# A two-layer attention kernel: value banks opened at the first value product, probabilities in order, the last key chunk token-major, matmul transposes at the barriers, roots of the layer norm on GpSimd

## The chip, the cores and the metric

The kernel runs on one core of one Trainium2 chip. The metric is the device time of one execution in microseconds (us). Every kernel was run four times. Of each the median is given, and a ratio to the kernel before, which was run in the same rounds on the same chip. A 95% interval of the ratio stands in square brackets.

The names in the profile are PE (TensorE, matrix products), PEld (its weight loads, which overlap products), ACT (ScalarE), DVE (VectorE), POOL (GpSimd) and SPq (the queue that issues most transfers). In the lines of the profile D and G are tiles in PSUM, the memory into which TensorE writes its products, X holds the residual, WA and WB are weights, and names that begin with p are tiles of the kernel's pools in SBUF, the on-chip memory for operands.

## The reference

There are two layers, and each is two blocks with a residual. Block A is causal attention in four segments of 512 tokens with 32 heads of 16 columns, plus a running memory. Block B is linear attention with a softmax feature map.

```python
x = x + A(layernorm(x));  x = x + B(layernorm(x))          # twice, x is [2048, 512]
# A, for each segment s of 512 tokens and each head:
p     = softmax(q_s @ k_s.T * 16**-0.5 + causal_mask)
a_dot = p @ v_s
a_mem = (phi(q_s) @ M) / (phi(q_s) @ z + 1e-6)
o_s   = g * a_mem + (1 - g) * a_dot
M, z  = M + phi(k_s).T @ v_s,  z + sum(phi(k_s))
# B, for each head; not causal: kv needs the keys of all 2048 tokens
phi_k = [softmax(k @ w_phi), softmax(-(k @ w_phi))]        # phi_q likewise
kv    = phi_k.T @ v;   z = sum(phi_k)
o     = (phi_q @ kv) / (phi_q @ z + 1e-6)
# layernorm: (x - mean) / sqrt(var + 1e-5), no weights
```

B's sum `kv` is a barrier. No query of B can be finished before the last token of A has gone through the residual, the layer norm and the key side of B. There is one such barrier in each layer.

## The kernel before

The kernel is a Python program that records operations with an estimated duration each. It plans them once, before the launch, and emits one fixed order of instructions for each engine. **The order of each engine stays as planned, whatever the real durations are.** A buffer is taken when the plan issues the first operation that "opens" it, and it comes free after its last reader. `CAPG` limits how many PSUM banks a class may hold at once: `pv` is the value tiles, `gen` the general ones.

```python
CAPG = {"gen": 3, "pv": 2, "nz": 1}

def ln(self, t, xT, flex=False):                    # layer norm of one tile of 128 tokens
    v(lambda e: e.bn_stats(...), 602, ...)          # DVE; the number is the plan's estimate in ns
    v(lambda e: e.bn_aggr(...), 75, ...)            # DVE
    # the root: exp(-0.5 * ln(var + eps)), two operations on ScalarE
    self.g.op({"act": (141.0, lambda e: e.activation(rs, self.mv[:, t, 1:2], ACT.Ln, bias=self.epsln[:, 0:1]))}, ...)
    self.g.op({"act": (141.0, lambda e: e.activation(rs, rs, ACT.Exp, scale=-0.5))}, ...)
    ...                                             # xn = (x - mean) * rstd on DVE
    self.tr(...)                                    # transpose of xn by DMA

def a_att(self, L, s, i):                           # attention of one tile of queries
    for hp in range(2):
        PV = self.T(self.pG, "pv")                  # one value tile: 16 heads, one PSUM bank
        for gg in range(2):
            for j in range(i + 1):
                # scores of 8 heads against 128 keys: two products of 512 columns
                self.mm(..., [512] * 2, ..., [S], opens=[PT, PV], label="S")
                self.act(..., ACT.Exp, 1024, [S], [PT], scale=0.25, label="exp")
                ...                                 # mask of the diagonal tile on GpSimd
            # ... value products, 17 columns each, from PT into PV
    ...                                             # divide, out-projection, residual
```

The key side of B (`b_keys`) works on a chunk of 512 tokens at once. It makes keys feature-major (one feature per partition, the tokens in a row), takes exponentials, transposes them by DMA, and then forms the values and `kv`. With the last chunk all of that lies behind the last token of A.

Of the kernel before, what the change touches and what calls it, by code (L numbers as in the profile page):

```python
# [9 lines left out]
ALU = mybir.AluOpType  # L10
# [470 lines left out]
class Kernel:  # L481
# [50 lines left out]

    def recip(self, e, o, i):

        with self.nc.allow_low_precision(reason="one softmax weight per key and head, kept in the operands' type"):
            return e.reciprocal(o, i)  # L536
# [6 lines left out]
    def alloc(self):  # L543
        nc, sb = self.nc, self.sb
        self.X = sb("X", [128, NT, D], BF16)
        self.WA = {k: sb(f"WA_{k}", [128, 4, D], BF16) for k in ("q", "k", "v", "o")}
        self.WB = {k: sb(f"WB_{k}", [128, 4, D], BF16) for k in ("q", "k", "v", "o")}
        self.ident = sb("ident", [128, 128], BF16)
        self.onesb = sb("onesb", [128, 128], BF16)
        self.eps8 = sb("eps8", [128, 8], BF16)  # L550
        self.epsln = sb("epsln", [128, 1], F32)
        self.ones8 = sb("ones8", [128, 8], F32)
        self.H8 = sb("H8", [128, 8], F32)
        self.H8b = sb("H8b", [128, 8], BF16)
        self.S4 = sb("S4", [128, 4], F32)
        self.A8 = sb("A8", [128, 8], F32)
        self.beta_sb = sb("beta_sb", [128, H], BF16)
        self.gt = sb("gt", [128, 3, H], F32)
        self.GAm = sb("GAm", [128, NG, 8, 17], F32)
        self.MS32 = sb("MS32", [128, NG, 8, 17], F32)  # L560
        self.MSb = [sb(f"MSb{b}", [128, NG, 8, 17], BF16) for b in range(3)]
        self.stats = sb("stats", [128, NT, 6], F32)
        self.mv = sb("mv", [128, NT, 2], F32)
        self.rstd = sb("rstd", [128, NT], F32)
        self.nb = sb("nb", [128, NT], F32)
        self.KV32 = sb("KV32", [128, 8, 136], F32)
        self.Rkv = sb("Rkv", [128, 8, 8, 16], BF16)
        self.Rz1 = sb("Rz1", [128, 8, 8, 2], BF16)
        self.wphi_st = sb("wphi_st", [128, NG, 16], BF16)

        def pool(name, n, shape, dt, caps=None, fifo=()):
            p = Pool(name, [sb(f"{name}{i}", shape, dt) for i in range(n)])
            p.caps = caps or {}
            p.fifo = fifo
            return p
        self.pX = pool("pX", N_XT, [128, 4, 512], BF16, {}, ("xA", "xB"))
        self.pQ = pool("pQ", N_Q4, [128, 4, 512], BF16, {}, ("Q4",))
        self.pK = pool("pK", N_KT, [128, 2, 512], BF16, {}, ("KT",))
        self.pV = pool("pV", 2, [128, 4, H, 17], BF16, {}, ("VT",))
        self.p1 = pool("p1", N_K1, [128, 512], BF16, CAP1, ("QT", "phiQ", "PhK", "phiKT", "E"))  # L580
        self.p2 = pool("p2", N_K2, [128, 1024], BF16, CAP2, ("ET", "EQ"))
        self.pT = pool("pT", N_VT, [128, 2, H, 17], BF16, {}, ("Vt",))
        self.pS = pool("pS", N_SM, [128, 256], F32)
        dbl = [self.es.enter_context(nc.psum_tensor(f"D{i}", [128, 1024], F32)) for i in range(2)]
        sgl = [self.es.enter_context(nc.psum_tensor(f"G{i}", [128, 512], F32)) for i in range(4)]
        self.pD = Pool("pD", dbl, psum=True)
        self.pG = Pool("pG", sgl, psum=True)
        self.pG.caps = CAPG
        self.pools = [self.pK, self.pX, self.pQ, self.pV, self.p1, self.p2, self.pT, self.pS, self.pD, self.pG]
# [5 lines left out]
    def setup(self):  # L595
# [34 lines left out]
        P = "pool"  # L630
        v(lambda e: e.memset(self.ones8[:], 1.0), 120, [], [R("ones8")], eng=P)
# [17 lines left out]
        v(lambda e: e.memset(self.epsln[:], LN_EPS), 70, [], [R("epsln")])  # L649
# [18 lines left out]
        for k in ("q", "k"):  # L668
            for g in range(NG):
                for hf in range(2):  # L670
                    c0 = g * 128 + hf * 64
                    self.evac(lambda k=k, c0=c0: self.WA[k][:, :, c0:c0 + 64].rearrange("p t (d s) -> p t d s", s=4),
                              lambda k=k, c0=c0: self.WAraw[k].t[:, :, c0:c0 + 64].rearrange("p t (s d) -> p t d s", s=4),
                              256, [self.WAraw[k]], [R("WP", k, g, hf)])
# [45 lines left out]
    def ln(self, t, xT, flex=False):  # L720
# [4 lines left out]

        rs = self.rstd[:, t:t + 1]
        self.g.op({"act": (141.0, lambda e: e.activation(rs, self.mv[:, t, 1:2], ACT.Ln, bias=self.epsln[:, 0:1]))},  # L727
                  [R("mv", t), R("epsln")], [R("rstd", t)], label="rstd")
        self.g.op({"act": (141.0, lambda e: e.activation(rs, rs, ACT.Exp, scale=-0.5))}, [R("rstd", t)], [R("rstd", t)], label="rstd")  # L729
# [12 lines left out]
        self.tr(lambda: xT.t[:, :, tt * 128:(tt + 1) * 128], lambda: xn.t[:], [xn], [xT[tt]], label="xnT")  # L742
# [84 lines left out]
    def a_att(self, L, s, i):  # L827
# [9 lines left out]
        for hp in range(2):  # L837
            PV = self.T(self.pG, "pv")
            pvv = lambda PV=PV: PV.t[:, 0:288].rearrange("p (h c) -> p h c", c=18)
            for gg in range(2):  # L840
# [3 lines left out]
                for j in range(i + 1):  # L844
# [5 lines left out]
                        [512] * 2, [KT[0], KT[1]] + Q4all(Q4), [S], opens=[PT, PV], label="S")  # L850
# [15 lines left out]
                if s >= 1:  # L866
# [4 lines left out]
                        [8, 8], [PQ, R("MSb", mb, hp), R("onesb"), R("eps8")], [PV[("d", gg)]], label="NMd")  # L871
# [13 lines left out]
        self.out_proj(t, o, [o[0], o[1]], self.WA["o"], R("WA", "o"))  # L885

    def out_proj(self, t, o, ores, W, wres, store=False, res_pe=False):
        R = self.R
        oT = self.T(self.p1, "oT")
        ps = self.T(self.pG, "gen")  # L890
        self.tr(lambda: oT.t[:].rearrange("p (a b) -> p a b", a=4), lambda: o.t[:], ores, [oT], label="otr")
# [12 lines left out]

    def b_keys(self, L, c):
        R, v = self.R, self.v
# [20 lines left out]
        for tt in range(4):  # L927
# [4 lines left out]
            ps = self.T(self.pG, "gen")  # L932
            self.vproj(ps, self.WB["v"], [R("WB", "v"), Vt["z"]], tt, xT, label="BV")
            v(lambda e, ps=ps, Vt=Vt: e.tensor_tensor(Vt.t[:, :, :, 0:16],  # L934
                                                      ps.t[:, None, 0:512].to_broadcast([128, 2, 512]).rearrange("p s (h d) -> p s h d", h=H),
                                                      Vt.t[:, :, :, 16:17].to_broadcast([128, 2, H, DH]), ALU.mult), 1131,
              [ps[0], Vt["z"]], [Vt["v"]], label="Vt")
        for q in range(3):
# [6 lines left out]
            n = len(slots)  # L945
            src = lambda ps=ps, n=n: ps.t[:, 0:136 * n].rearrange("p (k c) -> p k c", k=n)
            dst = lambda slots=slots, n=n: self.KV32[:, slots[0]:slots[0] + n, :]
            rd = [ps[0]]
            if c == 0:
                v(lambda e, src=src, dst=dst: e.tensor_copy(dst(), src()), 65 + 136 * n / 0.96, rd, [R("KV32", q)], label="KVacc")  # L950
            else:
                v(lambda e, src=src, dst=dst: e.tensor_tensor(dst(), dst(), src(), ALU.add), 65 + 136 * n / 0.96, rd + [R("KV32", q)],
                  [R("KV32", q)], label="KVacc")
            if c == 3:
                s0 = slots[0]
                kv = lambda s0=s0, n=n: self.KV32[:, s0:s0 + n, :].rearrange("p k (h c) -> p k h c", c=17)
                v(lambda e, kv=kv, s0=s0, n=n: e.tensor_tensor(self.Rkv[:, s0:s0 + n], kv()[:, :, :, 0:16],
                                                               self.H8[:, None, :, None].to_broadcast([128, n, 8, 16]), ALU.mult),
                  65 + 128 * n / 0.96, [R("KV32", q), R("H8")], [R("Rkv", q)], label="Rkv")
                v(lambda e, kv=kv, s0=s0, n=n: e.tensor_tensor(self.Rz1[:, s0:s0 + n, :, 0], kv()[:, :, :, 16],  # L960
                                                               self.H8[:, None, :].to_broadcast([128, n, 8]), ALU.mult),
                  90, [R("KV32", q), R("H8")], [R("Rz", q)], label="Rkv")

    def b_query(self, L, c, store):
# [36 lines left out]
        for tt in range(4):  # L1001
# [3 lines left out]
            o = self.T(self.p1, "o")  # L1005
# [3 lines left out]
                    [128] * 8, list(EQ.values()) + [R("Rkv", q) for q in range(3)], [N], opens=[Tm, o], label="N")  # L1009
# [4 lines left out]
            v(lambda e, Tm=Tm, o=o: e.tensor_tensor(o.t[:], Tm.t[:, 0:512], Tm.t[:, 512:1024], ALU.add), 335, [Tm], [o], label="nadd")  # L1014
            self.out_proj(t, o, [o], self.WB["o"], R("WB", "o"), store=store, res_pe=True)


    def build(self):
# [4 lines left out]
        def lnA(L, s):  # L1023
            self.xA[(L, s)] = self.T(self.pX, "xA")
            for t in range(s * 4, s * 4 + 4):
                self.ln(t, self.xA[(L, s)], flex=(L == 1))

        for L in range(2):
# [7 lines left out]
            for s in range(NSEG):  # L1036
# [7 lines left out]
                for i in range(4):  # L1044
                    self.a_att(L, s, i)
                    self.ln(s * 4 + i, self.xB[(L, s)])
                self.b_keys(L, s)
# [22 lines left out]
CAPG = {"gen": 3, "pv": 2, "nz": 1}  # L1070
ROUNDS = 5
# [38 lines left out]
```

## Time and profile before

The kernel before took 661.0 us (median of four runs in the rounds with the changed kernel, 658.42 to 666.8). Its profiled execution has a span of 654.6 us. I cut that span at four events, all read from the timeline: the first projection, the last value product of each layer, and the first normalising multiplication of B's query side in each layer, an operation of VectorE. Between the last value product and that multiplication lies the barrier.

| stage (us) | length |
|---|---|
| head: start to first projection | 21.1 |
| attention of layer 0 | 234.1 |
| barrier of layer 0 | 37.7 |
| queries of B, then attention of layer 1 | 267.5 |
| barrier of layer 1 | 36.7 |
| tail: queries of B of layer 1 | 57.5 |

This is part 1 of the page of the kernel before, busy time of each engine:

```profile
PE 548.8 (84%) x5728; PEld 292.3 (45%) x5728; DVE 433.0 (66%) x901; ACT 480.9 (73%) x705; POOL 157.1 (24%) x155
```

The table of engine time by stretch of the kernel before gives, for each stage after the head, its length, the busy time of each engine with the number of instructions, and the granted clock of TensorE (the number after the POOL entry):

```profile
core 0: us, PE busy (x) PEld busy (x) DVE busy (x) ACT busy (x) POOL busy (x), PEclk, DMA share, GB/s
21.10:255.20 234.10, 209.80 (x2317) 112.29 (x2318) 157.04 (x333) 201.44 (x287) 70.54 (x65) 0.96 0.31 64
255.20:292.90 37.70, 28.32 (x270) 15.48 (x266) 23.26 (x41) 12.93 (x18) 0.00 (x0) 0.91 0.35 64
292.90:560.40 267.50, 242.08 (x2581) 127.94 (x2582) 183.16 (x392) 228.82 (x333) 70.53 (x64) 0.98 0.28 53
560.40:597.10 36.70, 25.55 (x252) 14.38 (x250) 23.04 (x41) 9.03 (x14) 0.00 (x0) 0.91 0.38 69
```

In the barrier nothing is full. These lines are from the timeline of the kernel before, the barrier of layer 0: start, duration, engine, line, operation, count, and in brackets the idle time before it with the releaser.

```profile
254.85 0.40 PE L508 MATMUL G<-pV,p 128*128 128x17 bf16 x10
...
261.11 1.03 PE L508 MATMUL G<-WA_o,p 128*128 128x512 bf16 x4
...
265.38 0.29 ACT L727 ACTIVATE rstd<-mv,epsln 128x1 f32<-128x1 f32 x1 [3.92 <-DVE mv L724]
265.62 1.02 ACT L514 ACTIVATE p<-D 128x1024 bf16<-128x1024 f32 x1
266.54 0.19 ACT L729 ACTIVATE rstd<-rstd 128x1 f32<-128x1 f32 x1
...
267.51 0.40 DVE L739 TENSOR_SCALAR p<-X,mv,rstd 128x512 bf16<-128x512 bf16 x1
...
270.72 3.61 PE L508 MATMUL D<-pX,WB_k 128*128 128x512 bf16 x16 [0.73 <-DMA pX<-p]
...
277.78 6.55 PE L508 MATMUL G<-WB_v,pX 128*128 128x512 bf16 x16 [0.66 <-DVE pT L536]
...
285.74 2.05 PE L508 MATMUL G<-pT,p 128*128 128x136 bf16 x32 [1.41 <-DVE pT L934]
...
289.00 0.96 PE L508 MATMUL G<-Rz,p 128*128 128x16 bf16 x32 [1.21 <-DVE Rz L960]
```

From the last value product to the first sum of the queries (`Rz`) it takes 33.8 us (255.2 to 289.0). The second half of the root, at 266.54, queued behind an exponential of something else. The 16 value projections at 277.78 took 6.55 us, 0.41 us each, about twice the densest pitch, at a granted clock of 0.5. The Trainium skill, "TensorE: Matmul & The Clock Gate", Part 1, says that the array falls to half its clock after an idle window of about 3.4 us; the trace agrees in the size of the step.

Last come the exponentials of the attention of layer 0, from the groups of instructions of the kernel before in 21.1 to 255.2 us: count, busy time, mean ns of one, then the idle time before them and what ended it.

```profile
L514 ACT ACTIVATE p<-D 128x1024 bf16<-128x1024 f32 x171 | 165.7, 1032 | 19.5 <-PE D L508 18.9
```

ScalarE waited 18.9 us in this stretch for scores.

### The profile page before, as it was taken

What the parts mean: (1) busy time and instruction counts of PE and PEld (TensorE: products, weight loads), DVE (VectorE), ACT (ScalarE), POOL (GpSimd) and SP (SyncE); (2) the same over time, 40 slices, a digit from 0 to 9 for tenths busy, and PEclk for the clock granted to TensorE, in tenths of its full rate; (3) what the DMA queues carried; (4) which work ended last, traced back from release to release, by engine and by line L of the source; (5) the groups of instructions that cost most, each with busy time, mean ns of one, the idle gap of its engine ahead of it and who ended that gap; (6) DMA issues with size and microseconds to landing.
All of it is one profiled execution on the core that took longest, in us unless ns stands there. A gap on an engine that the chain in (4) does not pass through costs nothing.

```text
span 654.6 us, 13817 instructions
## 1 busy us (share of the span) xinstructions
PE 548.8 (84%) x5728; PEld 292.3 (45%) x5728; DVE 433.0 (66%) x901; ACT 480.9 (73%) x705; POOL 157.1 (24%) x155
## 2 busy tenths in 40 slices
PE   0479888898899999668998888989897999876885
PEld 0224444544545555334554434544453555334442
DVE  8666867767665764577799767756563776556454
ACT  4479979898887998305888979999898789421532
POOL 6321324333323421000002333333222342000000
PEclk9969989999999999988999999999999999887978
DMA  5923322212510422423333422212321241341323
GB/s 125 313 61 66 62 52 59 43 33 65 75 33 17 71 46 42 72 42 60 71 77 79 80 49 49 53 34 53 80 29 25 34 66 27 74 72 38 70 75 87
DMA packets 129006, 41.83 MB, mean 64 GB/s; under 512 B 120080, under 2 KB 127792, under 8 KB 128944
## 3 DMA queue, kind: packets, MB, share of 16 engines
q1 hardware_dynamic: 127584, 36.21, 28.5%
q0 software_dynamic: 1360, 4.74, 2.3%
q8 instruction: 45, 0.74, 0.5%
q14 instruction: 17, 0.14, 0.1%
HBM read 6.32 MB, written 2.10 MB: 13 GB/s over the span
## 4 chain that ended last, share of the span: by engine, by line
PE 49%; ACT 25%; DVE 15%; DMA 7%; issue 2%; POOL 1%; SPq 1%; ACTq 0%
PE G L508 30%; ACT p L514 22%; PE D L508 19%; DMA p<-p 3%; DVE p L1010 3%; DMA pX<-p 2%; DVE pT L934 2%; DVE p L739 1%; POOL p L854 1%; DMA pQ<-p 1%; DVE stats L723 1%; DVE p L757 1%; DVE pK L522 1%; DVE pT L536 1%; ACT pS L514 1%
## 5 line engine op out<-in xcount | busy, mean ns | idle before, releaser
L514 ACT ACTIVATE p<-D 128x1024 bf16<-128x1024 f32 x384 | 373.1, 1030 | 82.8 <-PE D L508 80.9
L854 POOL TENSOR_SCALAR_AFFINE_SELECT p<-p 128x1024 bf16<-128x1024 bf16 x128 | 140.7, 1104 | 395.7 <-ACT p L514 395.6
L508 PE MATMUL D<-pQ,pK 128*128 128x512 bf16 x640 | 185.5, 386 | 21.8 <-ACT p L514 17.1
L508 PEld LDWEIGHTS G<-pV,p 128*128 128x128 bf16 x2656 | 85.4, 96 | 36.4 <-POOL p L854 11.7
L508 PE MATMUL G<-pV,p 128*128 128x17 bf16 (+1 forms) x2656 | 90.0, 173 | 8.6 <-POOL p L854 5.8
L508 PEld LDWEIGHTS D<-pQ,pK 128*128 128x128 bf16 x640 | 48.3, 98 | 88.9 <-ACT p L514 54.9
L508 PE MATMUL G<-pX,WA_k 128*128 128x512 bf16 x128 | 34.5, 395 | 24.0 <-DMA pX<-p 21.1
L536 DVE RECIPROCAL pS<-G 128x32 f32<-128x32 f32 (+1 forms) x64 | 20.5, 321 | 37.4 <-PE G L508 37.0
L723 DVE BATCH_NORM_STATS2 stats<-X 128x6 f32<-128x512 bf16 x64 | 43.4, 681 | 1.5 <-ACT X L521 0.4
L900 DVE TENSOR_TENSOR X<-X,G 128x512 bf16<-128x512 bf16 x32 | 21.9, 686 | 33.6 <-PE G L508 33.6
L934 DVE TENSOR_TENSOR pT<-G,pT 128x1024 bf16<-128x1024 f32 x32 | 38.5, 1214 | 7.0 <-PE G L508 6.7
L508 PE MATMUL G<-WA_o,p 128*128 128x512 bf16 x128 | 34.1, 390 | 6.2 <-DMA p<-p 4.0
L508 PE MATMUL G<-WA_v,pX 128*128 128x512 bf16 x128 | 35.1, 403 | 4.9 <-ACT p L521 2.3
L508 PE MATMUL G<-WB_v,pX 128*128 128x512 bf16 x128 | 36.8, 433 | 2.3 <-DVE pT L536 2.3
L508 PE MATMUL D<-pX,WB_q 128*128 128x512 bf16 x128 | 35.4, 425 | 4.0 <-DVE p L1010 3.6
L1010 DVE TENSOR_TENSOR p<-D,pS 128x1024 bf16<-128x1024 f32 x32 | 37.8, 1215 | 0.3
L739 DVE TENSOR_SCALAR p<-X,mv,rstd 128x512 bf16<-128x512 bf16 x48 | 26.2, 552 | 16.9 <-ACT rstd L729 16.9
L522 DVE CAST pK<-G 64x512 bf16<-64x512 f32 x42 | 28.9, 687 | 10.8 <-PE G L508 6.3
L508 PE MATMUL G<-WB_o,p 128*128 128x512 bf16 x128 | 34.8, 396 | 0.0
L727 ACT ACTIVATE rstd<-mv,epsln 128x1 f32<-128x1 f32 x64 | 18.6, 295 | 19.7 <-DVE mv L724 19.5
L508 PE MATMUL G<-pX,WA_q 128*128 128x512 bf16 x128 | 32.3, 386 | 0.1
L536 DVE RECIPROCAL pT<-G 128x64 bf16<-128x64 f32 x32 | 17.9, 559 | 21.3 <-PE G L508 20.9
(110 smaller groups left out, 683.1 us busy)
## 6 DMA issues: line engine op xcount, KB each, us to landing
pQ<-p SPq DMA_DIRECT2D x128, 32.0 KB, 1.8
p<-p SPq DMA_TRANSPOSE x152, 2.5
out_dram<-X SPq DMA_DIRECT2D x16, 128.0 KB, 1.7
X<-in_A_x_dram POOLq DMA_DIRECT2D x3, 512.0 KB, 8.7
pX<-p SPq DMA_TRANSPOSE x64, 2.5
pX<-in_B_wqkv_dram POOLq DMA_DIRECT2D x2, 512.0 KB, 8.7
X<-in_A_x_dram SPq DMA_DIRECT2D x4, 128.0 KB, 2.5
pX<-in_A_wk_dram SPq DMA_DIRECT2D x1, 512.0 KB, 3.9
```

Source lines behind the costliest of these rows:

```text
L508: ins = e.matmul(out_ap, lhsT, rhs, start=st, stop=sp, tile_position=(basep(lhsT), basep(out_ap)))
L514: return self.g.op({"act": (dur, lambda e: e.activation(out_ap(), in_ap(), func, scale=scale))}, reads, writes, opens, label=label)
L522: "dve": (n / 0.96 + 65, lambda e: e.tensor_copy(out_ap(), in_ap()))}
L536: return e.reciprocal(o, i)
L723: v(lambda e: e.bn_stats(self.stats[:, t, :], self.X[:, t, :]), 602, [R("X", t)], [R("st", t)], label="bn")
L727: self.g.op({"act": (141.0, lambda e: e.activation(rs, self.mv[:, t, 1:2], ACT.Ln, bias=self.epsln[:, 0:1]))}, [R("mv", t), R("epsln")], [ ...
L739: v(lambda e: e.tensor_scalar(xn.t[:], self.X[:, t, :], self.mv[:, t, 0:1], self.rstd[:, t:t + 1], op0=ALU.subtract, op1=ALU.mult), 300, [ ...
L757: v(lambda e: e.tensor_scalar(e_.t[:], e_.t[:], 1.0, None, op0=ALU.min), 202, [e_], [e_], label="phmin")
L854: v(lambda e, pt8=pt8: e.affine_select(pt8(), pt8(), [[0, 8], [1, 128]], ALU.is_ge, 0.0, base=0, channel_multiplier=-1), 1080, [PT], [PT], ...
L900: self.v(lambda e: e.tensor_tensor(self.X[:, t, :], self.X[:, t, :], ps.t[:, 0:512], ALU.add), 602, [R("X", t), ps[0]], [R("X", t)], label ...
L934: v(lambda e, ps=ps, Vt=Vt: e.tensor_tensor(Vt.t[:, :, :, 0:16], ps.t[:, None, 0:512].to_broadcast([128, 2, 512]).rearrange("p s (h d) -> ...
L1010: v(lambda e, tt=tt, N=N, Tm=Tm: e.tensor_tensor(Tm.t[:].rearrange("p (s h d) -> p s h d", s=2, h=H), N.t[:].rearrange("p (s h d) -> p s h ...
```

## The change

Its intent has five parts. (1) A value bank is opened at the first value product and no longer at the first score product, so scores and exponentials can run ahead. To keep this safe from deadlock, probabilities (`PT`) and value banks are taken in program order. (2) The last chunk of B's keys is made token-major, in two parts, tokens 0 to 383 and then 384 to 511, so that only the last tile should be left behind the barrier. (3) On the latency chains, transposes are done by TensorE with a copy out of PSUM, not by DMA. (4) The roots of the layer norm move from ScalarE to GpSimd, as an add and a power. (5) Weights are permuted group by group, in the order in which the first projections use them.

```diff
     def ln(self, t, xT, flex=False, pe=False):
-        self.g.op({"act": (141.0, lambda e: e.activation(rs, self.mv[:, t, 1:2], ACT.Ln, bias=self.epsln[:, 0:1]))},
-                  [R("mv", t), R("epsln")], [R("rstd", t)], label="rstd")
-        self.g.op({"act": (141.0, lambda e: e.activation(rs, rs, ACT.Exp, scale=-0.5))}, [R("rstd", t)], [R("rstd", t)], label="rstd")
+        v(lambda e: e.tensor_scalar(rs, self.mv[:, t, 1:2], LN_EPS, None, op0=ALU.add), 100,
+          [R("mv", t)], [R("rstd", t)], eng="pool", label="rstd")
+        v(lambda e: e.tensor_tensor(rs, rs, self.mhalf[:], ALU.pow), 120,
+          [R("rstd", t), R("mhalf")], [R("rstd", t)], eng="pool", label="rstd")
...
+        if pe:
+            self.tpe(dst, lambda: xn.t, [xn], [xT[tt]], [xT], label="xnT")   # 4 PE transposes and a copy
+        else:
+            self.tr(dst, lambda: xn.t[:], [xn], [xT[tt]], label="xnT")
...
-        self.p2 = pool("p2", N_K2, [128, 1024], BF16, CAP2, ("ET", "EQ"))
+        self.p2 = pool("p2", N_K2, [128, 1024], BF16, CAP2, ("ET", "EQ", "PT"))
+        self.pG.fifo = ("pv",)
...
-                        [512] * 2, [KT[0], KT[1]] + Q4all(Q4), [S], opens=[PT, PV], label="S")
+                        [512] * 2, [KT[0], KT[1]] + Q4all(Q4), [S], opens=[PT], label="S")
...
+    def b_keys_tok(self, L, c, parts):
+        for part in parts:
+            for tt in part:
+                self.vproj(S, self.WB["k"], [...], tt, xT, opens=[E, Z], label="BK")
+                for sgn in range(2):
+                    self.act(..., ACT.Exp, 512, ..., label="kexp")
+                    v(fn, 598, [E[sgn]], [Z[sgn]], label="Zred")      # sum over the 16 columns of a head
+                ...                                                   # reciprocal, value products, scaling
+            for q in range(3):
+                self.mm(..., label="KV")                              # kv of this part, then added
...
+TOK = {3: ((0, 1, 2), (3,))}
+PE_T = ({("xA", 0, t) for t in range(4)} | {("xB", L, 15) for L in range(2)} | {("a", L, 15) for L in range(2)}
+        | {("b", 0, t) for t in range(4)} | {("xA", 1, t) for t in range(4)} | {("b", 1, 0), ("b", 1, 15)})
```

Cut are the helper of the PE transposes, the pair form of the last out-projections (transpose and sum in one product), and the loop order of the permutes.

## The prediction

> **What bounds it.** The table of engine time by stretch shows two regimes. In the attention stretches (50-257 us and 345-558 us) ScalarE is busy 184 of 207 us and 191 of 213 us; four back-to-back 128x1024 exponentials take 3.68 us (timeline), 0.92 us each, and 320 of them are 294 of those 420 us. TensorE busy is about as high (190 and 192 us) but inflated by pipelining: dense pairs of 512-column products start 0.22 us apart, so it has slack. Around the barriers (257-310, 558-601) and in the tail no engine is full: it is a latency chain at a granted clock of 0.87-0.88. Value products run 0.43 us apart there, twice the dense pitch. The Trainium skill, "TensorE: Matmul & The Clock Gate", Part 1, says an idle stretch of about 3.4 us halves the clock; this trace agrees.
>
> **Barrier (twice).** From the last value product (255.3 us): DMA transpose of o, Wo, LN, DMA transpose of xn (2.5 us each plus issue), 16 key products, exponentials and sums, 16 cold value products, 4 Vt of 1.2 us, 32 KV products, done at 287.7. The change leaves only token tile 15 after the barrier: 4+4 products, 2 half exponentials (0.61 us), 2 reductions (0.65 us each, estimate from same-sized DVE work), a reciprocal 0.56, one Vt, 8 KV products. The key part falls from 17 us to about 8. Two PE transposes with evacuation (4 transposes 0.4 us, copy 0.4-0.6) save some 1.5 us each; roots on Pool stop queueing behind key exponentials (Ln at 265.38, Exp at 266.54). The work for tiles 12-14 moves into busy attention. Net gain about 10 us per barrier, 20 in all.
>
> **Head.** First product waits to 21.1 us for a DMA transpose that took 6.8 us while loads ran. PE transposes plus group-ordered permutes bring it to about 16; the Q4 DMAs still meet the loads. Gain 4 us. Risk: Pool memsets (1.8 us each, 3.6-8.9 us) stand before the roots.
>
> **Layer boundary and tail.** Transposes of x and of the first and last outputs: 4 us together.
>
> **Attention.** A root pair costs ScalarE about 0.29 us of issue spacing, not its 0.50 us of durations; 44 pairs in the attention stretches give 13 us. Not opening the value bank at S lets S and exp run ahead and frees a bank for projections: ScalarE waits for S 34 us there; I expect 8-10 us back. Minus some 6 us of work moved in: net gain 16 us.
>
> Sum: 20+4+4+16 = 44 us.
>
> **Predicted time 617 us**, 80% range 600 to 639; faster by over 2% 0.93, within 2% 0.06, slower 0.01.
>
> **What the profile would show.** Barrier: first query sums 10 us sooner after the last value product, granted clock above 0.9, KV products in groups of 24 and 8. Head: first projection at 15-17 us. Attention: ScalarE 92% or more busy, no roots on it, each stretch 7-9 us shorter, exp waiting for S well below 34 us; Pool has 128 more instructions under 0.5 us. Tail: the last product follows the last nmul without a DMA.
>
> **What would make it wrong.** A slow power on Pool (1 us or more), or roots stuck behind masks in Pool's order. The Trainium skill, "SBUF — State Buffer", Who interferes with whom, says Pool and VectorE lock a shared port; the trace fits it (two xn took 2.70 us while a Pool memset ran, normally 0.55 each). Probabilities in order may cost freedom. The static schedule is rebuilt whole, so a few us may shift anywhere. If attention is bound by the exp-mask-value chain rather than ScalarE, the 16 us shrink to a few.

## More of the kernel before

In the attention stages TensorE is busy for 90% of the time (209.80 of 234.10) and ScalarE for 86% (201.44). Both figures overstate the load, because a record is longer than the time after which its engine starts the next instruction. At its densest, TensorE starts 512-column products 0.216 us apart, while a single record of one is 0.38 us long. I therefore count TensorE work another way: each weight load stands for a product, and each product is charged its densest pitch in the trace (0.216 us for 512 columns, 0.026 us for 17). By that estimate the attention of layer 0 holds 188 us of TensorE work in 234 us (80%), and the following stage holds 223 us in 267.5 us (83%). ScalarE is about as full by a like estimate: its exponentials of 1024 columns have records of 1.03 us and start 0.90 us apart at the densest, so the 171 of layer 0's attention come to 154 us, and with the 36 us of its other records to 190 us in 234 (81%).

## The result and the profile after

The changed kernel took 633.91 us (629.29 to 634.63), with a ratio of 0.9564 [0.9485, 0.9643] to the kernel before. A ratio compares the fast runs of both kernels round by round, so it is not quite the ratio of the medians. The gain is 27 us by the medians and 21.8 us by the two profiled spans (654.6 and 632.8). The stages add up to the spans, so the 21.8 us are what the tables split.

| stage (us) | before | after | difference | predicted |
|---|---|---|---|---|
| head | 21.1 | 15.9 | −5.2 | −4 |
| attention of layer 0 | 234.1 | 237.6 | +3.5 | −7 to −9 |
| barrier of layer 0 | 37.7 | 23.0 | −14.7 | −10 |
| queries, attention of layer 1 | 267.5 | 274.3 | +6.8 | −7 to −9, and part of the −4 below |
| barrier of layer 1 | 36.7 | 23.0 | −13.7 | −10 |
| tail | 57.5 | 59.0 | +1.5 | part of −4 |

The latency chains gained more than predicted. The attention, which was to give 16 us, cost 10 us.

This is part 1 of the page after, and then from part 5 of that page the groups of the roots and of the operation that waits for them:

```profile
PE 535.4 (85%) x5680; PEld 301.4 (48%) x5760; DVE 461.3 (73%) x932; ACT 466.9 (74%) x586; POOL 211.3 (33%) x285
...
L741 POOL TENSOR_SCALAR rstd<-mv 128x1 f32<-128x1 f32 x64 | 15.6, 246 | 151.8 <-DVE mv L739 151.2
...
L754 DVE TENSOR_SCALAR p<-X,mv,rstd 128x512 bf16<-128x512 bf16 x48 | 32.9, 688 | 16.0 <-POOL rstd L743 15.4
...
L743 POOL TENSOR_TENSOR rstd<-rstd,mhalf 128x1 f32<-128x1 f32 x64 | 37.8, 594 | 4.1
```

The power took 594 ns of GpSimd and the add 246 ns, where the plan of the change counted 120 and 100. ScalarE lost 119 instructions and 14 us of busy time. The records of 80 of 5760 products are missing (x5680 against x5760 loads), which is why products are counted by their loads here.

The table of engine time by stretch after, cut at the same events:

```profile
core 0: us, PE busy (x) PEld busy (x) DVE busy (x) ACT busy (x) POOL busy (x), PEclk, DMA share, GB/s
15.90:253.50 237.60, 214.12 (x2394) 119.67 (x2426) 184.18 (x375) 198.96 (x237) 100.24 (x129) 0.98 0.35 73
253.50:276.50 23.00, 14.62 (x140) 8.77 (x137) 14.54 (x33) 7.84 (x12) 0.79 (x2) 0.76 0.00 1
276.50:550.80 274.30, 247.81 (x2681) 139.37 (x2722) 204.97 (x414) 223.75 (x278) 95.45 (x126) 0.97 0.29 52
550.80:573.80 23.00, 14.58 (x138) 8.72 (x135) 14.51 (x34) 7.80 (x12) 0.79 (x2) 0.76 0.00 1
```

ScalarE is now busy for 84% and 82% of the attention stages (86% both times before), and for 89% from 60 to 253 us, a stretch more like the one that I predicted 92% for. TensorE has 108 and 140 more weight loads there (2318 to 2426, 2582 to 2722). At the densest pitch the added products are 12 and 11 us of work by the estimate above. VectorE gained 27 and 22 us of busy time.

The timeline of the barrier of layer 0 after, to be laid beside the one of before:

```profile
252.60 0.96 PE L508 MATMUL G<-pV,p 128*128 128x17 bf16 x32
...
256.05 0.39 PE L540 MATMUL G<-ident,p 128*128 128x128 bf16 x4
...
257.67 1.03 PE L508 MATMUL G<-WA_o,p 128*128 128x512 bf16 x4
...
261.03 0.22 POOL L741 TENSOR_SCALAR rstd<-mv 128x1 f32<-128x1 f32 x1 [9.02 <-DVE mv L739]
261.33 0.57 POOL L743 TENSOR_TENSOR rstd<-rstd,mhalf 128x1 f32<-128x1 f32 x1
261.93 0.41 DVE L754 TENSOR_SCALAR p<-X,mv,rstd 128x512 bf16<-128x512 bf16 x1 [0.99 <-POOL rstd L743]
262.40 0.40 PE L540 MATMUL G<-ident,p 128*128 128x128 bf16 x4 [1.96 <-DVE p L754]
...
263.32 1.04 PE L508 MATMUL G<-WB_k,pX 128*128 128x512 bf16 x4 [0.52 <-DVE pX L522]
...
266.99 1.89 PE L508 MATMUL G<-WB_v,pX 128*128 128x512 bf16 x4 [2.64 <-DVE pT L548]
...
270.20 1.09 PE L508 MATMUL G<-pT,p 128*128 128x136 bf16 x8 [1.32 <-DVE pT L963]
...
272.53 1.02 PE L508 MATMUL G<-Rz,p 128*128 128x16 bf16 x32 [1.24 <-DVE Rz L955]
```

From the last value product (253.6) to the first `Rz` product it is now 19.0 us, 14.8 us sooner than before. On the chain that decides are now only four key products, four value projections and eight `kv` products. Four value projections and 24 `kv` products of the first part also come after the last value product (254.3 to 259.6), but they fill the wait for the last tile. The last value projections still run cold. The table by stretch, cut finer inside this barrier, shows when the clock falls:

```profile
262.40:265.00 2.60, 1.43 (x8) 0.53 (x8) 0.42 (x1) 0.76 (x2) 0.00 (x0) 1.00 0.00 0
265.00:267.00 2.00, 0.01 (x1) 0.01 (x1) 1.88 (x3) 0.60 (x1) 0.00 (x0) 0.65 0.00 0
267.00:269.00 2.00, 1.88 (x4) 0.42 (x4) 0.08 (x1) 0.00 (x0) 0.00 (x0) 0.50 0.00 0
```

It drops to 0.50 during the sums and the reciprocal, and it stays there to the end of the barrier. The mean clock of the barrier fell from 0.91 to 0.76, although I had predicted above 0.9. This goes with a TensorE that is busy for less of the barrier (14.62 of 23.00 us, 64%, against 28.32 of 37.70 us, 75%). That this is the cause was not tested.

The exponentials of the attention of layer 0 after, from the groups in 15.9 to 253.5 us:

```profile
L514 ACT ACTIVATE p<-D 128x1024 bf16<-128x1024 f32 x173 | 168.2, 1029 | 25.0 <-PE D L508 24.1 <-PE G L508 0.2
```

The wait for scores rose from 18.9 to 24.1 us, where I had predicted a clear fall.

### The profile page after: what moved, and what is told of

The parts are those of the page before. It is cut to its first block, busy times and chain, and to the rows that moved or that the text cites. A ratio compares the mean times of both kernels' runs of the same rounds, so it can differ in the third digit from the quotient of the medians.

```text
span 632.8 us, 13820 instructions
## 1 busy us (share of the span) xinstructions
PE 535.4 (85%) x5680; PEld 301.4 (48%) x5760; DVE 461.3 (73%) x932; ACT 466.9 (74%) x586; POOL 211.3 (33%) x285
## 4 chain that ended last, share of the span: by engine, by line
PE 42%; DVE 34%; ACT 9%; POOL 6%; DMA 5%; issue 3%; SPq 0%; POOLq 0%
PE G L508 24%; PE D L508 16%; ACT p L514 7%; DVE p L1086 3%; DMA p<-p 3%; DVE stats L738 3%; DVE pK L522 3%; DVE p L754 3%; DVE p L782 3%; POOL rstd L743 2%; DVE X L933 2%; DVE p L776 2%; POOL p L873 1%; DVE p L893 1%; DVE p L522 1%
## 5 line engine op out<-in xcount | busy, mean ns | idle before, releaser
L514 ACT ACTIVATE p<-D 128x1024 bf16<-128x1024 f32 x376 | 366.9, 1030 | 75.6 <-PE D L508 73.2
L508 PE MATMUL D<-pQ,pK 128*128 128x512 bf16 x640 | 181.8, 382 | 13.6 <-ACT p L514 6.7
L741 POOL TENSOR_SCALAR rstd<-mv 128x1 f32<-128x1 f32 x64 | 15.6, 246 | 151.8 <-DVE mv L739 151.2
L514 ACT ACTIVATE p<-G 128x512 bf16<-128x512 f32 x64 | 38.8, 607 | 8.6 <-PE G L508 4.1
L754 DVE TENSOR_SCALAR p<-X,mv,rstd 128x512 bf16<-128x512 bf16 x48 | 32.9, 688 | 16.0 <-POOL rstd L743 15.4
L522 DVE CAST pK<-G 64x512 bf16<-64x512 f32 x52 | 35.5, 684 | 6.0 <-PE G L508 5.3
L743 POOL TENSOR_TENSOR rstd<-rstd,mhalf 128x1 f32<-128x1 f32 x64 | 37.8, 594 | 4.1
L508 PE MATMUL G<-WB_v,pX 128*128 128x512 bf16 x114 | 31.5, 396 | 7.6 <-DVE pT L548 5.3
L508 PE MATMUL G<-WA_v,pX 128*128 128x512 bf16 x119 | 32.4, 402 | 3.1 <-DVE nb L748 1.2
L508 PE MATMUL D<-pX,WB_q 128*128 128x512 bf16 x122 | 31.2, 393 | 3.2 <-DVE p L1086 3.0
```

What stands on the lines that cost most here:

```text
L508: ins = e.matmul(out_ap, lhsT, rhs, start=st, stop=sp, tile_position=(basep(lhsT), basep(out_ap)))
L514: return self.g.op({"act": (dur, lambda e: e.activation(out_ap(), in_ap(), func, scale=scale))}, reads, writes, opens, label=label)
L522: "dve": (n / 0.96 + 65, lambda e: e.tensor_copy(out_ap(), in_ap()))}
L743: v(lambda e: e.tensor_tensor(rs, rs, self.mhalf[:], ALU.pow), 120, [R("rstd", t), R("mhalf")], [R("rstd", t)], eng="pool", label="rstd")
L754: v(lambda e: e.tensor_scalar(xn.t[:], self.X[:, t, :], self.mv[:, t, 0:1], self.rstd[:, t:t + 1], op0=ALU.subtract, op1=ALU.mult), 300, [ ...
```

## The experiments

Twelve kernels were run, four in each of three calls. The medians of the kernel before in the three were 662.46, 662.61 and 659.21 us. Where kernels of different calls are compared, differences below some 4 us are not read. Two theories stood against each other for the attention.

- **The TensorE theory.** TensorE is the limit there: the moved work costs what it weighs, and relieving ScalarE gives nothing.
- **The GpSimd theory.** The roots on GpSimd hurt by themselves and hide the gain, through the shared port that the prediction names, or through their place in an order that was planned with too short an estimate.

Both can hold a part, so the runs are to tell how much each holds. The expectations are quoted as they were before each run, with the names and guesses of that moment. The first four runs undo one part of the change each.

### Roots back on ScalarE (u_roots)

```diff
-        v(lambda e: e.tensor_scalar(rs, ..., op0=ALU.add), 100, ..., eng="pool")
-        v(lambda e: e.tensor_tensor(rs, rs, self.mhalf[:], ALU.pow), 120, ..., eng="pool")
+        self.g.op({"act": (141.0, ... ACT.Ln, bias=self.epsln ...)}, ...)
+        self.g.op({"act": (141.0, ... ACT.Exp, scale=-0.5 ...)}, ...)
```

> The change with the roots on ScalarE again. My prediction's reckoning: 44 root pairs at 0.29 us come back on ScalarE in attention, so about 10 us slower, 640 to 646 us. Theory M: ScalarE is not what holds attention, so within 4 us of the changed kernel. Theory P (the roots on Pool cost as much as they free: power 0.59 us each where the schedule counts 0.12, and VectorE's normalising op 0.69 us on average against 0.55): a few us faster, 625 to 632 us.

It took 620.58 us (615.96 to 621.63), ratio 0.9357 [0.93, 0.9414]. With the roots back on ScalarE the kernel is 13 us faster than with them on GpSimd. By stages of its profile, the barriers are 4.0 and 3.6 us longer than after the change. In layer 0 the roots' queue on ScalarE explains about 1.5 us of this: from the end of the variance to the normalisation of the last tile it takes 2.5 us (253.0 to 255.6), against 1.0 us after the change (260.9 to 261.9). Most of the rest is key-side work that this order leaves behind the last value product, as the barrier holds 185 weight loads against 134. The head is 3.7 us shorter (12.2), and the two attention stages are 5.4 and 13.3 us shorter (232.2 and 261.0). So the offload, predicted at +13 us, was worth −13 with the plan as written.

### Value bank opened at the scores again (u_open)

```diff
-                        ..., [S], opens=[PT], label="S")
+                        ..., [S], opens=[PT, PV], label="S")
-        ..., CAP2, ("ET", "EQ", "PT"))        # and self.pG.fifo = ("pv",) is gone
+        ..., CAP2, ("ET", "EQ"))
```

> The change with the value bank opened at S and probabilities in any order again. My prediction's reckoning: 8 to 10 us come back, 642 to 646 us, all of it in the attention stretches, where exp waits more for S. Rival (running ahead is worth little because TensorE is full): within 4 us. Rival (running ahead is what pays for the moved work): 15 us or more slower.

It took 681.58 us (680.62 to 683.75), ratio 1.0298 [1.0235, 1.0361]: 48 us slower than the changed kernel and slower than the kernel before. All of it is in the attention (269.9 and 288.7 us). Barriers, head and tail are within 0.2 us of those after. Late opening was not worth the 8 to 10 us of the prediction but nearly five times that, in this company.

### Key chunk feature-major again (u_tok)

```diff
-TOK = {3: ((0, 1, 2), (3,))}
+TOK = {}
```

> The change with the last key chunk channel-major again (all else changed). Theory M (moved work): the last chunk's token-major form takes work out of the barriers and puts it into the two attention stretches, which are held by TensorE work at its dense pitch (188 to 201 us of a 234 to 238 us stretch, counted from the weight loads), so here each barrier (last value product to first normalising product of the query side, 23.0 us after) grows by 9 to 12 us, and each attention stretch (237.6 and 274.3 us after) shrinks by 5 to 8 us; total 638 to 645 us. Rival (lost gain has nothing to do with moved work): barriers grow by 10, attention stays within 2 us, total about 654 us.

The ratio was 0.9737 [0.9673, 0.9801] over its three fast runs (642.35, 645.25 and 646.91 us). Against 0.9564 that is 0.0173 of 661 us, so 11 us. The profiled run was a slow one (652.66 us), so its stages are only a hint: barriers of 33.8 and 33.0 us against 23.0, and 5 us less in the stage of layer 1's attention. If the 21 us at the barriers hold for fast runs too, the token-major form gives about half of them back elsewhere. The slow run shows only 5 us of that, so the split is not shown.

### No PE transposes (u_pet)

```diff
-PE_T = ({("xA", 0, t) for t in range(4)} | ...)
+PE_T = set()
```

> The change with all transposes on DMA again. My prediction's reckoning: 4 us of the head, some 3 us of each barrier and 4 us at the boundary and tail come back, 14 us, 645 to 650 us, with the first projection near 20 us and barriers of 26 us. Rival (PE transposes save latency only in the head and barriers, the tail gains nothing): 640 to 645 us, tail unchanged at 59 us.

Three runs took 636.19, 639.68 and 639.7 us, ratio 0.9642 [0.958, 0.9703]. All PE transposes together are thus worth some 6 us, less than the parts of the prediction that rest on them suggested. The fourth run, the profiled one, took 2785 us. Its granted clock is given as 1.0, but that says nothing, as this trace holds no record of the clock at all (that of the kernel before holds 24). In the groups of instructions of that run a score product's record is 1679 ns long, where 380 to 390 ns are usual:

```profile
L508 PE MATMUL D<-pQ,pK 128*128 128x512 bf16 x640 | 915.4, 1679 | 0.0
```

Its 512-column products start 1.28 us apart in the median (0.216 us in the other runs), while an exponential had its usual length (1023 ns). So TensorE was slow and ScalarE was not, and a lower clock of TensorE that was not recorded can't be ruled out. The cause was not found, the run was left out, and the stages of this kernel could not be read.

### Dead GpSimd work beside the good schedule (pool_dummy)

This is `u_roots` with the order of every other engine kept. After planning, the same add and power, on constants and with results that nobody reads, are put into GpSimd's order after each `bn_aggr`.

```diff
+        for o in self.g.order:                       # after the schedule is made
+            order.append(o)
+            if o in self.aggr:                       # each bn_aggr
+                # on GpSimd: dead = ones + eps ; dead = dead ** -0.5
+                order += [a, b]
```

> The kernel with the roots on ScalarE (620.6 us), every engine's order kept, and after each statistics op the two small Pool ops run as well, on constants, with a result that nobody reads. Theory L (the port and Pool's strict order: Pool ops in the way of VectorE's bf16 ops and of the masks): 626 us or more, and the mean of VectorE's normalising op rises from 0.50 us towards 0.69. Theory D (the chain through Pool is slow for those who wait for the root, or the static order was planned with 0.12 us for a 0.59 us power): within 3 us of 620.6.

It took 624.19 us (621.71 to 625.64), ratio 0.9412 [0.9375, 0.9449], against 0.9357 [0.93, 0.9414] of `u_roots`. The intervals overlap, and the medians differ by 3.6 us. From its groups of instructions:

```profile
L1148 POOL TENSOR_TENSOR dead<-dead,mhalf 128x1 f32<-128x1 f32 x64 | 38.3, 598 | 5.3
...
L757 DVE TENSOR_SCALAR p<-X,mv,rstd 128x512 bf16<-128x512 bf16 x48 | 22.9, 485 | 12.9 <-ACT rstd L747 12.7
```

GpSimd does the same work (598 ns a power), and VectorE's normalisation is no slower for it: 485 ns, against 502 in `u_roots` and 688 after the change. Occupying GpSimd, or a port that VectorE shares with it, is not what costs 13 us. That part of the GpSimd theory falls. What is left of it is the longer way through GpSimd to the normalisation, and the place of the roots in the orders of the engines. The next run keeps the first and changes the second.

### Two numbers of the plan put right (r_pcal)

```diff
-        v(... op0=ALU.add), 100, ..., eng="pool")
+        v(... op0=ALU.add), 220, ..., eng="pool")
-        v(... ALU.pow), 120, ..., eng="pool")
+        v(... ALU.pow), 570, ..., eng="pool")
```

> The change with the two root ops on Pool planned at what the trace shows (0.22 and 0.57 us in place of 0.10 and 0.12). Theory D in its planning form: the schedule allows for them, 620 to 626 us. Theory L: no better than the change, 630 to 637 us. A new schedule alone may move a few us either way.

It took 622.88 us (619.31 to 625.77), ratio 0.9398 [0.9355, 0.944]. The roots stay on GpSimd and no instruction is added or removed. Only the plan knows that they are long, and 11 of the 13 us are back. Its profile has 234.3 and 267.1 us of attention against 237.6 and 274.3, by the table of engine time by stretch (columns as above):

```profile
15.70:250.00 234.30, 209.62 (x2386) 118.68 (x2422) 181.91 (x367) 200.81 (x243) 99.54 (x129) 0.99 0.37 74
...
275.00:542.10 267.10, 244.05 (x2676) 139.41 (x2718) 198.76 (x412) 221.40 (x275) 96.60 (x126) 0.97 0.29 54
```

So the loss lay in the static order: made with powers of 0.12 us, run with powers of 0.59 us. A rebuilt schedule may by itself shift by some 8 us (see `roots_nofifo`), so the size is less sure than the sign: two schedules with the true plan took 622.88 and 614.74 us, two with the short one 633.91 and 634.94 us, the latter two nearly alike. With a true plan the roots on GpSimd and the roots on ScalarE (0.9357 [0.93, 0.9414]) can't be told apart in this pair. Here taking 64 root pairs off ScalarE bought nothing, which is what the TensorE theory says. A second pair below (`pcal_nofifo` and `roots_nofifo`) says otherwise.

Not settled is where in the order the loss sits. I looked for it in VectorE's normalisation, whose mean fell from 688 to 578 ns here. But in `pcal_nofifo` below it is 620 ns in a kernel that is faster still.

### Late opening alone (a_open)

This is the kernel before with part (1) of the change and nothing else.

> The kernel before with nothing but the late opening of the value bank, with probabilities in order. My prediction's reckoning: 8 to 10 us faster than before, so 651 to 654 us. Undoing it in the change cost 48 us; if that holds here too, 612 to 620 us. If late opening pays mostly because the other parts filled attention with work, something like 640 to 650 us. Barriers stay near 37 us in all three.

It took 648.18 us (644.05 to 651.62), ratio 0.9779 [0.972, 0.9839]: 14 us faster, though the interval does not clear 2%. The attention stages lost 9.0 and 11.8 us and the barriers grew by 3.4 and 4.2, probably because more of the key side is left over when the attention ends sooner (in layer 1 the barrier holds 270 weight loads against 250, in layer 0 only 270 against 266). The wait for scores in layer 0, from the groups in 21.3 to 246.4 us:

```profile
L514 ACT ACTIVATE p<-D 128x1024 bf16<-128x1024 f32 x170 | 164.6, 1036 | 16.5 <-PE D L508 15.5 <-PE G L508 0.6
```

It fell from 18.9 to 15.5 us, so the direction of the prediction was right. That is 3.4 of the 9.0 us by which the stage became shorter. Another 4.8 us of ScalarE's waits went where it copies projected values and keys out of PSUM (4.2 to 1.3 us and 10.8 to 8.9 us in the same view), which fits the bank that late opening leaves to the projections.

### A third value bank with the early opening (open_pv3)

If early opening hurts because only two value tiles may be under way, then a third bank must give much of it back. If it hurts by the order alone, a third bank gives little.

```diff
# u_open, and:
-CAPG = {"gen": 3, "pv": 2, "nz": 1}
+CAPG = {"gen": 3, "pv": 3, "nz": 1}
```

> The value bank opened at S as in the kernel before, in any order, but three value banks allowed in place of two (of the four single banks), all else as in the change (681.6 us so, 633.9 late). If what hurts is that only two head pairs of heads can be under way, a third gives back 15 to 35 us: 647 to 667 us. If it is the banks that the projections lack while value banks are held idle, a third makes it no better or worse: 678 us or more.

It took 653.99 us (653.25 to 654.81), ratio 0.987 [0.9845, 0.9895]: 27.6 of the 48 us are back, and 20 us are not. The exponentials of layer 0's attention in the groups of `u_open` (15.9 to 285.8 us):

```profile
L514 ACT ACTIVATE p<-D 128x1024 bf16<-128x1024 f32 x178 | 171.5, 1032 | 38.8 <-PE D L508 38.3
```

And in those of `open_pv3` (15.9 to 264.9 us):

```profile
L514 ACT ACTIVATE p<-D 128x1024 bf16<-128x1024 f32 x176 | 169.6, 1028 | 25.6 <-PE D L508 25.1
```

The wait for scores was 38.3 us with two banks and 25.1 us with three. A value tile that is claimed at its first score blocks the scores of the tile after next. Freeing that is more than half of what late opening is good for here. Where the other 20 us lie was not tested. The third bank comes out of the same four single banks that the projections use, and the forced order is missing as well.

### The old weight order (u_perm)

The permutes run again over all groups of q and then of k, each free to go to ScalarE or VectorE by the general copy helper, with its shorter estimates.

```diff
-        for g in range(NG):
-            for k in ("k", "q"):
+        for k in ("q", "k"):
+            for g in range(NG):
```

> The change with the weight permutes in their old order; roots on Pool still planned at 0.12 us. It undoes the last part of the change and gives a second schedule with the short plan. My prediction's reckoning: at most 2 us of the head come back. If the short plan is what costs (theory D, planning form), this one is slow as well: 630 to 640 us. If the 11 us between the change and the run with corrected durations were the luck of one schedule, this one may lie anywhere between 618 and 640 us.

It took 634.94 us (632.24 to 635.35), ratio 0.9624 [0.9557, 0.9691]. The head is 16.4 us against 15.9, and all other stages lie within some 2.5 us of those after. The weight order is worth next to nothing. I had also meant it as a second schedule with the short plan, to see whether the 11 us of `r_pcal` could be luck. The schedule turned out so close to that of the change that it says little about this.

### True plan, and no forced order (pcal_nofifo)

```diff
# r_pcal, and:
-        ..., CAP2, ("ET", "EQ", "PT"))
-        self.pG.fifo = ("pv",)
+        ..., CAP2, ("ET", "EQ"))
```

> Roots on Pool planned at measured durations, and probabilities and value banks in any order. A second schedule with the right plan: if the plan is the cause, 617 to 626 us. The order by itself: no effect expected beyond 4 us, since late opening needs it only against a stuck plan, and no plan got stuck.

It took **614.74 us** (611.82 to 617.63), ratio 0.9326 [0.9254, 0.9397]. This is the fastest kernel: 19 us below the changed one by the medians and 16 by the ratios, with intervals that don't touch (0.9564 [0.9485, 0.9643]). Its attention stages are 230.4 and 260.4 us. Against `r_pcal`, the medians differ by 8 us and the ratios by 0.007, with overlapping intervals. It was run at another time.

### No forced order, roots on ScalarE (roots_nofifo)

```diff
# u_roots, and:
-        ..., CAP2, ("ET", "EQ", "PT"))
-        self.pG.fifo = ("pv",)
+        ..., CAP2, ("ET", "EQ"))
```

> Roots on ScalarE, and probabilities and value banks in any order; the candidate for the fastest. Against the run with roots on ScalarE (620.6 us): if the order costs freedom, 612 to 618 us; if not, within 3 us.

It took 622.56 us (618.21 to 625.44), ratio 0.9439 [0.9361, 0.9517], against 0.9357 of `u_roots`. Here dropping the order brought nothing and perhaps cost a few us. So whether "probabilities in order" costs anything is not settled: dropping it gave minus 8 us in one company and plus 2 in the other, by the medians. I take this as the size by which a rebuilt schedule may shift without any one cause.

The run also gives a second pair for the roots: on GpSimd with a true plan 614.74 us, on ScalarE 622.56 us, and no run of the one is as slow as any of the other (at most 617.63, at least 618.21). By the profiles the attention stages are 4.7 and 2.5 us shorter with the roots on GpSimd. So without the forced order the move of the roots seems to have brought some 8 us, and with it nothing. What relieving ScalarE is worth stays open between these two.

### All but late opening and GpSimd roots (roots_open)

This keeps the token-major chunk, the PE transposes and the weight order only. It is `u_roots` with the edit of `u_open`.

> Token-major last chunk, PE transposes and weight order alone: roots on ScalarE, value bank opened at S, any order. If the parts add up, it is before less 28 us of barriers and 5 of the head plus some 12 us of work moved into attention: 640 to 645 us, and late opening is worth 20 to 25 us here (as it was 14 alone). If early opening turns the moved work into loss whoever does the roots, 660 us or more, and late opening is worth 40 us or more.

It took 653.59 us (649.55 to 658.68), ratio 0.9918 [0.9811, 1.0026]. These parts cut both barriers and the head and yet hardly beat the kernel before. This run makes the path from before to after a sum of three steps, each from two profiled runs:

| stage (us) | before | token-major, PE transposes, weight order (roots_open) | then late opening and order (u_roots) | then roots on GpSimd, short plan (after) | after |
|---|---|---|---|---|---|
| head | 21.1 | −8.8 | −0.1 | +3.7 | 15.9 |
| attention of layer 0 | 234.1 | **+12.8** | **−14.7** | +5.4 | 237.6 |
| barrier of layer 0 | 37.7 | −10.9 | +0.2 | −4.0 | 23.0 |
| queries, attention of layer 1 | 267.5 | **+13.8** | **−20.3** | **+13.3** | 274.3 |
| barrier of layer 1 | 36.7 | −10.8 | +0.7 | −3.6 | 23.0 |
| tail | 57.5 | +1.5 | +1.9 | −1.9 | 59.0 |
| span | 654.6 | −2.3 | −32.4 | +12.9 | 632.8 |

The first step takes 22 us out of the barriers and 9 out of the head, and puts 27 us into the attention. The work that it moved there was 9 and 10 us at the densest pitch, and its price was 13 and 14 us. In that order it found no free time on TensorE.

The same three parts can be read once more with late opening in place, from `a_open` to `u_roots`: the barriers lose 14.1 and 14.3 us, the head 9.1, and the attention stages gain only 7.1 and 5.3 us (225.1 to 232.2, 255.7 to 261.0) for 7 and 10 us of work. So the price is not simply the weight, which speaks against the TensorE theory in its plain form. With early opening the moved work cost more than its weight, with late opening about three quarters of it, and the three parts together were worth 28 us by the medians (648.18 to 620.58; 23.5 us by the two profiled spans) instead of 5 or 6.

The second step of the table, late opening, thus pays for the first. The steps don't simply add: late opening is worth 14 us alone, 33 us here and 48 us beside badly planned roots, and a badly planned GpSimd root costs 13 us with late opening and 28 us without it (681.58 against 653.59; by the ratios the 33 are 37 and the 28 are 25, as the runs are of different calls). A kernel that can't run ahead passes every lateness on.

## Why the prediction was right, and which of its steps were not

The time, 633.91 us, lies in the predicted range of 600 to 639 and is faster by over 2%, as given at 0.93. The predicted 617 was 17 us too low. The sum "20+4+4+16 = 44" holds in its direction and not in its terms. That the time fell into the range was partly luck: barriers and head gave 34 us where 24 were predicted, and this hid an attention that cost 10 us where it was to give 16.

- **Barrier, "net gain about 10 us per barrier".** It was right in its mechanism and too small: 14.7 and 13.7 us measured. Some 11 us of each came with the token-major chunk and the PE transposes. The other 4 us came with the step that put the roots on GpSimd: about 1.5 us of it is ScalarE's queue, most of the rest less key-side work left over. The sign in the profile was wrong, though: the granted clock went to 0.76 and not above 0.9.
- **Head, "gain 4 us".** 5.2 us. The risk that I named there was real: GpSimd clears buffers at the start, and the power of the fourth tile had to wait behind a clear of 1.80 us (its add ended at 10.15, the power began at 11.87). One normalisation took 2.05 us during that clear, against 0.41 us for one alone, but that is no cost of the change: in the kernel before one took 2.39 us during the clears. Without roots on GpSimd the head was 3.7 us shorter still.
- **Layer boundary and tail, "4 us together".** Nothing was seen at the tail (+1.5 us). The boundary can't be told from the attention around it. All PE transposes together were worth some 6 us, and how these are spread could not be read, as that profile was the 2785 us run.
- **Attention, "net gain 16 us".** This is the step that failed: +10 us. It had three terms.
  - *"44 pairs in the attention stretches give 13 us"*: with the plan as written the move cost 13 us. With a true plan the roots on GpSimd and on ScalarE are level in one pair (0.9398 and 0.9357), and in the other GpSimd is 8 us ahead (614.74 and 622.56 us). So relieving ScalarE gave between nothing and 8 us, not 13. "A slow power on Pool" stood among the things that would make the prediction wrong, with 1 us as the mark. 0.59 us was enough, not because GpSimd ran out of time (its busy share is 33%), but because the plan held 0.12 us.
  - *"I expect 8-10 us back"* from late opening: 14 us alone, 33 us in the company of the other parts. The mechanism, too few value tiles under way, was shown by the third bank for 28 of the 48 us that it was asked about.
  - *"Minus some 6 us of work moved in"*: by its weight it was 12 and 11 us. Its price was 13 and 14 us with early opening (`roots_open`), and 7 and 5 us with late opening (`a_open` to `u_roots`). I had inferred "it has slack" from the pitch without counting the work. The count leaves 20% and 17%, and how much of that can be had depends on the order.

I had also written that if the attention is bound by the chain of exponential, mask and value "rather than ScalarE, the 16 us shrink to a few". Without late opening the attention only lost. Which engine, if any, is the limit there was not shown. For TensorE speaks the fastest kernel, which reaches 87% and 89% of the densest pitch in its two attention stages, where the kernel before had 80% and 83%. But ScalarE was about as full before (81% in layer 0), the price of the moved work changed with the order, and no run makes TensorE faster. What the runs do show is that the order decides: late opening and a true plan moved the attention by more than any work taken off an engine.

Open are: what limits the attention; where in the order the short plan loses its 11 us; whether the forced order of the probabilities costs anything; and why one run took 2785 us.

## What to carry to other kernels

In a kernel with a static schedule, the estimated durations are part of the program: before moving an operation to another engine, measure it there, since a wrong 0.12 us for 0.59 us cost 11 us, about what the move was to bring. Before calling an engine free, count its work at its densest pitch and compare that with the stage, as work moved off a latency chain is not gone: here it cost 27 us where it went, against 22 us saved at the barriers, and 12 us against 28 once the order let the engines run ahead. And claim a scarce buffer at the first operation that writes it, not at the start of the chain that will fill it.

## What the Trainium skill lacked or had wrong

- **Power on GpSimd** ("GPSIMD Engine Reference"): § 3.1 times an add of 2048 columns and names two software dispatch hops, but has no figure for a power or for a one-column operand. Measured on 128x1: 594 ns for the power with a tensor exponent, 246 ns for an add of a constant (64 of each).
- **Sharing of the port** ("SBUF — State Buffer", § Who interferes with whom): the lock that it describes fits the start of the kernel (one normalisation of 2.05 us during a clear of 1.80 us, 0.41 us alone). It has no measure of what small operands cost: 128 one-column GpSimd operations added to a running kernel changed the time by 3.6 us by the medians, with overlapping intervals (`pool_dummy`, 0.9412 against 0.9357), and the mean normalisation not at all (485 against 502 ns).
- **Pitch of 512-column products** ("TensorE: Matmul & The Clock Gate", § Back-to-back issue gap): it gives about 131 ns as the measured sustained spacing and about 216 ns as the isolated one, though Part 1 of the page has 215.7 ns for back-to-back products as well. Here the densest stretches, with a weight load for each product, ran at 216 ns and never below 214. For the densest work of this kernel the "isolated" formula was the right one.
- **What counts as an idle window** (same page, Part 1): the halved clock is as told (0.50 in the barrier, four value projections in 1.89 us). But in the barrier after the change no gap before a TensorE instruction was longer than 2.64 us, and yet the clock fell at about 265.6 us (it averages 0.65 over 265 to 267 us); two groups of work, four transposes of 0.40 us and four products of 1.04 us, lay in the 3.4 us before. Nor is this special: of the 20 falls of the clock after 20 us in the two profiles, before and after, 19 followed 3.4 us in which TensorE was busy for 0.6 to 1.9 us. The page, with an idle window of about 3.4 us, doesn't say how much work inside such a window still counts as idle.
- **Transposes by TensorE** (same page, Part 4): about 275 ns for one in a kernel. Here four in a row took 0.39 to 0.40 us in the barrier (0.60 us in the head), and the copy out of PSUM 0.41 us on VectorE or 0.60 us on ScalarE; no page has that sum for a 128x512 tile.
